# Unit 0 of an attention and gated-MLP kernel: first loads on one queue, products of ones between its blocks, the last blocks scaled on VectorE, zeros beside k written first

## The chip, the cores and the metric

The kernel runs on one NeuronCore of a Trainium2 chip. The metric is the device time of one execution in microseconds, lower is better. Five engines have a queue of their own each and work in the order of that queue: TensorE (PE, with its weight loads shown as PEld), VectorE (DVE), ScalarE (ACT), GpSimd (POOL) and SyncE (SP), which here only issues DMAs. They wait for each other through semaphores. DMAs run beside them; in this kernel they are issued from SP and, at the start, from ACT.

## The reference

Windowed attention over 8 batches, 8 heads, 576 positions and head size 64 (heads 0 to 3 with a plain window of 32, heads 4 to 7 with the same window dilated by 4), and then an RMS norm and a gated MLP (512 to 1536 to 512) over all 4608 positions.

```python
scores = scale * np.matmul(q, k.transpose(0, 1, 3, 2))
scores = np.where(masks[None], scores, -1e9)
attn = np.exp(scores - scores.max(-1, keepdims=True))
attn_out = np.matmul(attn / (attn.sum(-1, keepdims=True) + 1e-9), v)
...
xn = x / np.sqrt(np.mean(x * x, -1, keepdims=True) + 1e-6) * rms_g
g, val = xn @ w_gate, xn @ w_val
out = (g / (1 + np.exp(-g)) * val) @ w_out
```

## The kernel before

The 4608 positions are cut into 16 units of 288 (half a batch). A unit's attention is 14 blocks `(c, i)`: `c` is a pair of heads (0 and 1 plain with 3 blocks each, 2 and 3 dilated with 4 each). A block needs, in this order, the scores `s` (PE, line 417 for units 0 and 1), their mask and row minimum (DVE, 312), the exponentials (ACT, 322), the reciprocal of the sum (DVE, 329 and 330), the scaling of both heads' rows (POOL, 332), a transposition `t` (PE, 394), its copy `pt` to SBUF (ACT, 374), the product with v, `o` (PE, 403), and a copy of that into `xraw` (ACT or DVE, 347). After a pair's last block, ACT squares `xraw` (355), POOL multiplies it by the norm's gain `gs` (357), and the squares are added (361). Behind the unit's last pair come the mean of the squares on PE (`rps`, 458), its root on DVE and POOL (465, 466), a diagonal matrix of it (490), and its spread over the partitions on PE (`bps`, 500), copied as `root` (505); the normalised rows `xn` (511) feed the MLP.

The order on every engine is written out by hand. The main function counts steps in `now`; `later(dt, rank, fn)` puts a piece of work off by `dt` steps, and `flush()` issues a step's pieces by rank. Unit 0's attention takes 25 steps ahead of the main loop (`for n in range(ends)`, lines 674 to 685): step n issues `t` of block n-4, `o` of block n-6 and `s` of block n, in this order on PE. So the transposition of block (1,1) stands in step 8, that of (3,2) in step 16 and that of (3,3) in step 17. From step 19 on the MLP's first products stand between them (`FIRST`, lines 39 and 681). The main loop then has 36 parts for each unit (12 columns of the hidden layer by gate, value and output product), with the next unit's attention in between.

Beside the attention the weights are decoded. They arrive as 36 pieces of 64-bit numbers (`raw_g`, `raw_v`, `raw_o`, 512 KB each, line 124), of which `NRAW` = 4 buffers hold what is under way. Each piece takes one conversion on ACT (135) and three operations on DVE (139, 142, 146), and then its buffer takes the next piece. The table `STEPS` (line 37) says how many of the 108 DVE operations each of the 25 first steps issues; the main loop issues three in each part until none is left.

q, k and v of unit 0 are loaded at the start, by `load(0, h)` for 8 heads (lines 639 and 640): q of a pair as one DMA (207), k of each head (212), v of a pair (218). The pairs 0 and 2 are loaded from SP's queue, the pairs 1 and 3 from ACT's, and behind them on ACT's the gain `gs` (641). The four first weight pieces follow on SP (642, 643). k of a head is padded with zeros in the other head's 64 partitions; a memset (211) does that just ahead of each k's load, on DVE for unit 0 and on POOL for unit 1, whose loads come at the steps 15, 19, 23 and 27.

DMAs from SP and ACT share eight completion counters, taken in turn. A DMA waits, at its place in the queue of its engine, until the earlier one with its counter has landed.

Of the kernel before, what the change touches and what calls it, by code (L numbers as in the profile page):

```python
# [9 lines left out]
F32 = mybir.dt.float32  # L10
# [4 lines left out]
ALU = mybir.AluOpType  # L15
PSUM = bass.MemoryType.PSUM

B, H, S, D = 8, 8, 576, 64
DM, FF = 512, 1536
NT = B * S  # L20
P = 128
U = S // 2
# [4 lines left out]
NC = DM // P  # L27
NJ = FF // P
NNAT = 2
NRAW = 4  # L30
KW = DIL * (U // DIL + W)
# [2 lines left out]


LAG, OUT, LATER = 4, 2, 1
STEPS = (0,) * 5 + (1,) + (2,) * 11 + (1, 1, 0, 0, 0, 1, 1, 1)
SPLITS = 30
FIRST = {19: (("g", 0), ("g", 1)), 20: (("g", 2),), 22: (("g", 3), ("v", 0), ("v", 1)),
         23: (("v", 2), ("v", 3))}  # L40
# [4 lines left out]
def geometry(u, c):  # L45


    half = u % 2
    if c < NC // 2:
        if half:  # L50
            return [(QB * i, QB * i, 0, P) for i in range(U // QB)], QB, U + W
        return [(QB * i, max(QB * i - W, 0), 0 if i else W, P if i else QB)
                for i in range(U // QB)], QB, U
    nq = U // DIL
    keys = nq + (W if half else 0)
    return [(nq * r, keys * r, 0 if half else W, keys) for r in range(DIL)], nq, keys * DIL
# [3 lines left out]
def attn_moe(ctx: ExitStack, tc: tile.TileContext, qk_in, v_in, w_gate, w_val, w_out, rms_g, outT):  # L60
# [3 lines left out]
    nc = tc.nc  # L64
    V, A, G, PE = nc.vector, nc.scalar, nc.gpsimd, nc.tensor

    cst = ctx.enter_context(tc.tile_pool(name="cst", bufs=1))
    sb = ctx.enter_context(tc.tile_pool(name="sb", bufs=2))
    ps = ctx.enter_context(tc.tile_pool(name="ps", bufs=1, space=PSUM))
# [6 lines left out]
    ones = cst.tile([P, P], F32R, name="ones")  # L76
# [11 lines left out]
    gs = cst.tile([P, NC], F32, name="gs")  # L88
# [9 lines left out]
    def later(dt, rank, fn):  # L98
        put_off.setdefault(now[0] + dt, []).append((rank, fn))

    def flush():
        for _, fn in sorted(put_off.pop(now[0], []), key=lambda e: e[0]):
            fn()
# [12 lines left out]
    def load_piece():  # L116
        n = state["loaded"]
        if n == len(pieces):
            return
        state["loaded"] += 1  # L120
        kind, j = pieces[n]
        raw = wp.tile([P, NC, P, 2], U32, tag="raw", name=f"raw_{kind}{j}", bufs=NRAW)
        src = {"g": w_gate, "v": w_val, "o": w_out}[kind][j]
        nc.sync.dma_start(out=raw.rearrange("p c f t -> p (c f t)"), in_=src)
        raws[n] = raw
# [34 lines left out]
    def decode(k):  # L160

        for _ in range(k):
            later(0, 5, step)
        if k:
            later(0, 5.2, ahead)
# [23 lines left out]

    heads, vs, late = {}, {}, []  # L190

    def load(u, h):


        c, a = divmod(h, 2)
        _, _, nkt = geometry(u, c)
        if u >= NNAT:
            raw = sb.tile([P, U + KW], F32, tag="qk", name=f"qk_{u}_{h}", bufs=2)
            nc.sync.dma_start(out=raw[:, :U + nkt], in_=qk_in[u, h][:, :U + nkt])
            heads[u, h] = raw  # L200
            return
        n = 4 * (u * NC + c)
        queue = A if u == 0 and c % 2 else nc.sync
        own, other = (slice(D), slice(D, P)) if a == 0 else (slice(D, P), slice(D))
        if a == 0:
            q = cst.tile([P, U], F32, tag=f"hi{n}", name=f"q_{u}_{c}")
            queue.dma_start(out=q, in_=qk_in[u, h:h + 2, :D, :U])
        else:
            q = heads[u, h - 1][0]
        k = cst.tile([P, KW], F32, tag=f"hi{n + 1 + a}", name=f"k_{u}_{h}")  # L210
        (G if u else V).memset(k[other, :nkt], 0.0)
        queue.dma_start(out=k[own, :nkt], in_=qk_in[u, h][own, U:U + nkt])
        heads[u, h] = q, k
        if a:
            blocks, _, _ = geometry(u, c)
            rows, cols = max(b[3] for b in blocks), len(blocks) * 2 * D
            vt = cst.tile([P, DIL, 2, D], F32, tag=f"hi{n + 3}", name=f"v_{u}_{c}")
            queue.dma_start(out=vt[:rows].rearrange("p i a d -> p (i a d)")[:, :cols],
                              in_=v_in[u, c][:rows, :cols])
            for i in range(len(blocks)):  # L220
                vs[u, c, i] = vt[:, i]
# [103 lines left out]
    def scores_norm(u, c, i):  # L325
        blocks, nq, _ = geometry(u, c)
        n = blocks[i][3]
        t, sm = st[u, c, i]
        V.tensor_scalar(out=sm[:nq, 2:4], in0=sm[:nq, 2:4], scalar1=1e-9, scalar2=None, op0=ALU.add)
        V.reciprocal(out=sm[:nq, 2:4], in_=sm[:nq, 2:4])  # L330
        for a in range(2):
            G.tensor_scalar(out=t[:nq, a, :n], in0=t[:nq, a, :n], scalar1=sm[:nq, 2 + a:3 + a],  # L332
                            scalar2=1.0, op0=ALU.mult, op1=ALU.mult)

    def take(u, c, i, o):

# [26 lines left out]
    def bursts(u):  # L363
        return [(u, c, i) for c in range(NC) for i in range(len(geometry(u, c)[0]))]
# [90 lines left out]
    def rms_sum(u):  # L455
        r_ps = ps.tile([QB, NB, 2], F32, tag="o", name=f"rps_{u}")
        for i in range(NB):
            PE.matmul(r_ps[:, i, :], xsq[u][:, i * QB:(i + 1) * QB], inv, start=True, stop=True)
        later(1, 0.1, lambda: rms_root(u, r_ps))
        if u == 0:  # L460
            later(1, 6, spread_first)
# [34 lines left out]
    def rms_apply(u):  # L496
        ds = rst.pop(u)
        b_ps = ps.tile([P, U], F32, tag="o", name=f"bps_{u}")
        for k, d in enumerate(ds):
            PE.matmul(b_ps, (ones if u else ones32)[:QB, :], d.rearrange("p i q -> p (i q)"),  # L500
                      start=k == 0, stop=k == len(ds) - 1)
        xs[u] = {}
        if u == 0:
            root.append(sb.tile([P, U], F32, tag="tmp", name="root", bufs=2))
            later(1, -1, lambda: A.copy(out=root[0], in_=b_ps))

        def normal(c):
            x = xraw[u, c]
            if u == 0:
                xn = sb.tile([P, U], F32, tag="xhi", name=f"xn_{c}", bufs=4)  # L510
                V.tensor_tensor(out=xn, in0=x, in1=b_ps, op=ALU.mult)
                xs[u][c] = xn
                return
            V.scalar_tensor_tensor(out=x, in0=x, scalar=gs[:, c:c + 1], in1=b_ps,  # L514
                                   op0=ALU.mult, op1=ALU.mult)

        def part(c):
            x = xraw.pop((u, c))
            k = (u * NC + c) % 6
            pool, bufs = (sb, 4) if k < 4 else (late[0], 2)  # L520
            hi = pool.tile([P, U], F32R, tag="xhi", name=f"xhi_{u}_{c}", bufs=bufs)
            lo = late[0].tile([P, U], F32R, tag="xlo", name=f"xlo_{u}_{c}", bufs=6)
            A.copy(out=hi, in_=x)
            (V if c % 2 else G).tensor_tensor(out=lo, in0=x, in1=hi, op=ALU.subtract)
            xs[u][c] = (hi, lo)

        for c in range(NC):
            later((1, 2, 2, 3)[c] if u else 1 + c // 2, 0.6, lambda c=c: normal(c))
            if u:
                later((2, 3, 4, 5)[c], 0.6, lambda c=c: part(c))  # L530
# [18 lines left out]
    def start(kind, c):  # L549

        if kind not in first:
            first[kind] = ps.tile([P, 512], F32, tag={"g": "acc1", "v": "acc3"}[kind], name=f"{kind}_0_0")
        three(first[kind][:, :U], weight(kind, 0, 0), c, xraw[0, c], c == 0, c == NC - 1)
# [82 lines left out]

    nb = len(bursts(0))
    ctx.enter_context(tc.manual_schedule())
    for h in range(H):
        load(0, h)  # L640
    A.dma_start(out=gs, in_=rms_g.rearrange("(c p) -> p c", p=P))
    for n in range(NRAW):
        load_piece()
    for h in range(H):
        later(15 + 4 * (h // 2), 9, lambda h=h: load(1, h))

# [9 lines left out]
    def attend(t_ps, **tags):  # L656
        e = events.pop(now[0], {})
        if any(k in e for k in "qto"):
            products(e.get("q"), e.get("t"), e.get("o"), t_ps, **tags)
        if "sum" in e:  # L660
            rms_sum(e["sum"])
        if "apply" in e:
            rms_apply(e["apply"])
# [10 lines left out]
    for n in range(ends):  # L674
        decode(STEPS[n])
        flush()
        t_ps = None
        if "t" in events.get(n, {}):
            t_ps = ps.tile([P, 512], F32, tag="gv"[n % 2], name=f"t_first_{n}")[:, :2 * QB]
        attend(t_ps, s_tag=("s", "acc0", "acc1", "acc3")[n % (4 if n < nb else 2)], o_tag=("o", "acc2")[n % 2])  # L680
        for kind, c in FIRST.get(n, ()):
            start(kind, c)
        if n == ends - 1:
            _, v_free = gate(0, 0), val(0, 0)
        now[0] += 1

    prev = None
    for u in range(NU):
        for j in range(NJ):
            for part in range(0 if u + j else 2, 3):  # L690
                t = 3 * (u * NJ + j) + part
# [94 lines left out]
```

## Time and profile before

| | us |
|---|---|
| median of 3 runs (lowest, highest) | 1195.87 (1193.26, 1196.34) |
| the profiled execution | 1192.86 |
| its span, first to last instruction | 1190.7 |
| PE busy, share of the span | 1140.4, 96% |
| DVE busy | 755.1, 63% |
| ACT busy | 676.4, 57% |
| POOL busy | 640.8, 54% |

In the lines quoted from the profile, a timeline row gives the start and the length in us, the engine, the line of the kernel, the operation with output and input tile, the shape, how many instructions were merged, and in brackets how long the engine was idle before it and what ended that. The engines SPq and ACTq stand for the issue of DMAs in the queues of SP and ACT. A row of a table by windows gives, for a stretch of time, its length and the busy time of each engine (with the number of instructions), then the clock granted to TensorE, the mean busy share of the 16 DMA engines, and GB/s.

### The profile page before, as it was taken

The numbers are of one execution on the slowest core, as the hardware profiler recorded it, in microseconds if no ns is written. First come the engines' busy times: TensorE is split into PE (matmuls) and PEld (weight loads), VectorE is DVE, ScalarE is ACT, GpSimd is POOL, SyncE is SP. The second block draws the span as 40 slices with busy tenths as digits, with TensorE's granted clock in tenths as the row PEclk, the third lists the DMA queues.
The fourth block names the chain that finished last, engine by engine and source line by source line (L and its number), as shares of the span: only waits on it lengthen the run. The fifth ranks groups of instructions, "written<-read, shape, count | busy, mean of one in ns | idle before, by whom it ended". The sixth has DMA issues, their size and how long they took to land.

```text
span 1190.7 us, 26009 instructions
## 1 busy us (share of the span) xinstructions
PE 1140.4 (96%) x8492; PEld 1103.2 (93%) x8492; DVE 755.1 (63%) x2715; ACT 676.4 (57%) x2456; POOL 640.8 (54%) x1094
## 2 busy tenths in 40 slices
PE   4788899999999999999999999999999999999998
PEld 3566688999999999999999999999999999999998
DVE  4789786765658576665857656585765757575321
ACT  4567576564646556474656646465665646565221
POOL 2666476664646555464655655465555645565211
PEclk9999899999999999999999999999999999999999
DMA  4555321121213112121312212131221213120000
GB/s 151 188 186 188 106 82 50 58 80 32 77 38 92 45 51 80 35 81 36 90 40 70 68 30 78 38 101 38 68 61 35 81 37 93 40 77 16 1 21 20
DMA packets 62711, 82.19 MB, mean 69 GB/s; under 512 B 7442, under 2 KB 43282, under 8 KB 62578
## 3 DMA queue, kind: packets, MB, share of 16 engines
q1 hardware_dynamic: 61242, 79.60, 21.9%
q8 instruction: 68, 1.11, 0.4%
q10 hardware_dynamic: 1336, 0.94, 0.3%
q14 instruction: 65, 0.53, 0.1%
HBM read 71.08 MB, written 9.44 MB: 68 GB/s over the span
## 4 chain that ended last, share of the span: by engine, by line
PE 78%; DVE 14%; DMA 2%; ACT 2%; issue 2%; POOL 1%; SPq 0%; POOLq 0%; DVEq 0%
PE acc L543 8%; PE acc L544 7%; PE acc L545 7%; PE v L543 7%; PE g L543 7%; PE v L544 7%; PE v L545 7%; PE g L544 7%; PE g L545 7%; PE s L420 3%; DVE qs L290 3%; PE g L394 2%; PE o L408 2%; PE o L409 2%; DVE xraw L514 2%
## 5 line engine op out<-in xcount | busy, mean ns | idle before, releaser
L607 POOL TENSOR_TENSOR hlo<-th,hhi 128x288 fp32r<-128x288 f32 x180 | 145.4, 808 | 218.3 <-ACT hhi L606 214.2
L332 POOL TENSOR_SCALAR t<-t,sm 96x128 f32<-96x128 f32 (+3 forms) x448 | 185.2, 425 | 99.4 <-DVE sm L330 74.1
L543 PE MATMUL v<-xhi,hi_v 128*128 128x288 f32 x720 | 220.3, 306 | 3.5 <-DVE pl L378 3.2
L543 PE MATMUL acc<-hhi,hi_o 128*128 128x288 f32 x720 | 221.1, 307 | 0.0
L543 PE MATMUL g<-xhi,hi_g 128*128 128x288 f32 x720 | 219.8, 305 | 0.0
L544 PE MATMUL acc<-hlo,hi_o 128*128 128x288 f32 x720 | 212.8, 295 | 0.2 <-POOL hlo L607 0.2
L544 PE MATMUL g<-xlo,hi_g 128*128 128x288 f32 x720 | 212.9, 296 | 0.0
L544 PE MATMUL v<-xlo,hi_v 128*128 128x288 f32 x720 | 212.8, 296 | 0.0
L545 PE MATMUL acc<-hhi,lo_o 128*128 128x288 f32 x720 | 212.6, 295 | 0.0
L545 PE MATMUL g<-xhi,lo_g 128*128 128x288 f32 x720 | 212.6, 295 | 0.0
L545 PE MATMUL v<-xhi,lo_v 128*128 128x288 f32 x720 | 212.3, 295 | 0.0
L322 ACT ACTIVATE t<-t,sm 96x128 f32<-96x128 f32 (+3 forms) x448 | 166.7, 375 | 18.4 <-DMA k<-in_qk_dram 13.6
L251 POOL TENSOR_TENSOR vlo<-vt,vhi 128x128 fp32r<-128x128 f32 x196 | 98.5, 502 | 125.2 <-ACT vhi L247 109.3
L577 ACT ACTIVATE th<-g 128x288 f32<-128x288 f32 x180 | 74.0, 411 | 157.7 <-PE g L545 106.2
L606 ACT CAST hhi<-th 128x288 fp32r<-128x288 f32 x180 | 78.0, 433 | 141.2 <-DVE th L595 137.2
L543 PEld LDWEIGHTS v<-xhi,hi_v 128*128 128x128 f32 x720 | 135.3, 188 | 6.5 <-DVE pl L378 6.5
L307 DVE TENSOR_TENSOR t<-s,mask 96x256 f32<-96x256 f32 (+3 forms) x196 | 72.0, 367 | 106.7 <-PE s L420 101.1
L544 PEld LDWEIGHTS acc<-hlo,hi_o 128*128 128x128 f32 x720 | 135.8, 189 | 0.5 <-POOL hlo L607 0.5
L544 PEld LDWEIGHTS g<-xlo,hi_g 128*128 128x128 f32 x720 | 135.7, 188 | 0.1
L544 PEld LDWEIGHTS v<-xlo,hi_v 128*128 128x128 f32 x720 | 135.7, 188 | 0.0
L543 PEld LDWEIGHTS acc<-hhi,hi_o 128*128 128x128 f32 x720 | 135.5, 188 | 0.0
L543 PEld LDWEIGHTS g<-xhi,hi_g 128*128 128x128 f32 x720 | 135.3, 188 | 0.2 <-issue 0.2
(120 smaller groups left out, 2662.0 us busy)
## 6 DMA issues: line engine op xcount, KB each, us to landing
qk<-in_qk_dram SPq DMA_DIRECT2D x56, 288.0 KB, 2.9
vt<-in_v_dram SPq DMA_DIRECT2D x196, 64.0 KB, 1.8
qk<-in_qk_dram SPq DMA_DIRECT2D x28, 352.0 KB
out_dram<-ot SPq DMA_DIRECT2D x64, 144.0 KB, 1.9
qk<-in_qk_dram SPq DMA_DIRECT2D x28, 304.0 KB, 2.7
raw_g<-in_w_gate_dram SPq DMA_DIRECT2D x12, 512.0 KB, 3.1
raw_v<-in_w_val_dram SPq DMA_DIRECT2D x12, 512.0 KB, 4.0
raw_o<-in_w_out_dram SPq DMA_DIRECT2D x12, 512.0 KB
```

Of the source, the lines that this page charges most:

```text
L251: G.tensor_tensor(out=vl, in0=vs.pop(b), in1=vh, op=ALU.subtract)
L290: eq.tensor_tensor(out=qs[D:], in0=qr[D:], in1=qs[D:], op=ALU.subtract)
L307: V.tensor_tensor(out=t[:nq, :, :n], in0=sv[:nq, :, 1, :n], in1=mask[:nq, None, mc:mc + n].to_broadcast([nq, 2, n]), op=ALU.add)
L322: A.activation(out=t[:nq, a, :n], in_=t[:nq, a, :n], func=AF.Exp, scale=-1.0, bias=sm[:nq, a:a + 1], accum_out=sm[:nq, 2 + a:3 + a])
L332: G.tensor_scalar(out=t[:nq, a, :n], in0=t[:nq, a, :n], scalar1=sm[:nq, 2 + a:3 + a], scalar2=1.0, op0=ALU.mult, op1=ALU.mult)
L420: PE.matmul(sv[:nq, a, :, :n], qs[:, qc:qc + nq], ks[:, :, kc:kc + n], start=True, stop=True)
L543: PE.matmul(out, wh[:, cc, :], xh, start=start, stop=False)
L544: PE.matmul(out, wh[:, cc, :], xl, start=False, stop=False)
L545: PE.matmul(out, wl[:, cc, :], xh, start=False, stop=stop)
L577: A.activation(out=t, in_=g, func=AF.Tanh, scale=0.5)
L606: A.copy(out=hi, in_=t)
L607: G.tensor_tensor(out=lo, in0=t, in1=hi, op=ALU.subtract)
```

## The change

Five things change, all of them in or ahead of unit 0's attention:

- All of q, k and v of unit 0 is loaded from SP's queue, in the order of the pairs, and `gs` behind the four first weight pieces.
- The zeros beside k of units 0 and 1 are written ahead of all loads, by a function `zeros`; on DVE for unit 0 and on POOL for unit 1 as before.
- A function `busy(n)` issues n products of a 128x128 tile of ones with 512 columns of it (float32r) into a PSUM tile that nobody reads: 7 ahead of the first scores, and 3 in each of the steps 0 to 17, behind that step's scores. The scores' PSUM tiles rotate among three instead of four, since the fourth now takes these products.
- For unit 0's blocks (3,1), (3,2) and (3,3) the scaling is done on DVE instead of POOL.
- `STEPS` issues no decoding in step 5 (one operation before), one in step 17, none in step 18 (one before); so 26 operations are done in the 25 steps, where 28 were.

```diff
-STEPS = (0,) * 5 + (1,) + (2,) * 11 + (1, 1, 0, 0, 0, 1, 1, 1)
+STEPS = (0,) * 6 + (2,) * 11 + (1, 0, 0, 0, 0, 1, 1, 1)
+BUSY = 7, 3
...
+    def zeros(u, h):
+        c, a = divmod(h, 2)
+        k = cst.tile([P, KW], F32, tag=f"hi{4 * (u * NC + c) + 1 + a}", name=f"k_{u}_{h}")
+        (G if u else V).memset(k[(1 - a) * D:(2 - a) * D, :geometry(u, c)[2]], 0.0)
+        zeroed[u, h] = k
...
-        queue = A if u == 0 and c % 2 else nc.sync
...
-            queue.dma_start(out=q, in_=qk_in[u, h:h + 2, :D, :U])
+            nc.sync.dma_start(out=q, in_=qk_in[u, h:h + 2, :D, :U])
...
-        (G if u else V).memset(k[other, :nkt], 0.0)
-        queue.dma_start(out=k[own, :nkt], in_=qk_in[u, h][own, U:U + nkt])
+        k = zeroed.pop((u, h))
+        nc.sync.dma_start(out=k[own, :nkt], in_=qk_in[u, h][own, U:U + nkt])
...
-            G.tensor_scalar(out=t[:nq, a, :n], in0=t[:nq, a, :n], scalar1=sm[:nq, 2 + a:3 + a],
-                            scalar2=1.0, op0=ALU.mult, op1=ALU.mult)
+            (V if u == 0 and (c, i) > (NC - 1, 0) else G).tensor_scalar(
+                out=t[:nq, a, :n], in0=t[:nq, a, :n], scalar1=sm[:nq, 2 + a:3 + a],
+                scalar2=1.0, op0=ALU.mult, op1=ALU.mult)
...
+    for u in range(NNAT):
+        for h in range(H):
+            zeros(u, h)
     for h in range(H):
         load(0, h)
-    A.dma_start(out=gs, in_=rms_g.rearrange("(c p) -> p c", p=P))
     for n in range(NRAW):
         load_piece()
+    nc.sync.dma_start(out=gs, in_=rms_g.rearrange("(c p) -> p c", p=P))
+    busy_ps = ps.tile([P, 512], F32, tag="acc3", name="busy")
+    def busy(n):
+        for _ in range(n):
+            PE.matmul(busy_ps, ones, ones[:, None, :].to_broadcast([P, 4, P]), start=True, stop=True)
+    busy(BUSY[0])
...
-        attend(t_ps, s_tag=("s", "acc0", "acc1", "acc3")[n % (4 if n < nb else 2)], o_tag=("o", "acc2")[n % 2])
+        attend(t_ps, s_tag=("s", "acc0", "acc1")[n % (3 if n < nb else 2)], o_tag=("o", "acc2")[n % 2])
+        if n < nb + LAG:
+            busy(BUSY[1])
```

On ACT the start reads as follows before the change. The names end in a running number that the build gives; `t_0_1` is block (0,1), `pt` a transposed block, `f_g` and `f_v` weight pieces under conversion, `raw_g` and `raw_v` what was loaded.

```order
L212 DMA k_3_108<-in_qk_dram 64x288
L218 DMA v_1_111<-in_v_dram 128x384
L207 DMA q_3_123<-in_qk_dram 128x1x288
L212 DMA k_6_125<-in_qk_dram 64x288
L212 DMA k_7_128<-in_qk_dram 64x288
L218 DMA v_3_131<-in_v_dram 72x512
L641 DMA gs<-in_rms_g_dram 128x4x1
L322 ACTIVATE t_0_0_145,sm_0_0_146<-t_0_0_145,sm_0_0_146 96x96 x2
```

After the change ACT's queue, from its third row on, holds this:

```order
L330 ACTIVATE t_0_0_172,sm_0_0_173<-t_0_0_172,sm_0_0_173 96x96 x2
L330 ACTIVATE t_0_1_182,sm_0_1_183<-t_0_1_182,sm_0_1_183 96x128 x2
L330 ACTIVATE t_0_2_198,sm_0_2_199<-t_0_2_198,sm_0_2_199 96x128 x2
L383 COPY pt_0_0_233<-t_first_220 96x192
L330 ACTIVATE t_1_0_214,sm_1_0_215<-t_1_0_214,sm_1_0_215 96x96 x2
L383 COPY pt_0_1_254<-t_first_241 128x192
L330 ACTIVATE t_1_1_235,sm_1_1_236<-t_1_1_235,sm_1_1_236 96x128 x2
L136 ACTIVATE f_g_262<-raw_g_149 128x512
L136 ACTIVATE f_v_266<-raw_v_151 128x512
L383 COPY pt_0_2_283<-t_first_268 128x192
```

No DMA is left on ACT, and the conversions of the first two weight pieces stand behind the copy of block (0,1) and the exponentials of (1,1); before, they stood ahead of both (behind the exponentials of (1,0)).

On PE the steps 8 and 9 of unit 0's attention now read as follows; before, they were the same rows without those of `busy`.

```order
L403 MATMUL t_first_327<-ident,t_1_1_235 128x96 x2
L412 MATMUL o_0_2_329<-pt_0_2_283,v_0_129 128x192
L426 MATMUL s_2_2_328<-k_4_101,q_2_137 72x72
L426 MATMUL s_2_2_328<-k_5_103,q_2_137 72x72
L661 MATMUL busy<-ones 128x512 x3
L403 MATMUL t_first_356<-ident,t_1_2_256 128x96 x2
L412 MATMUL o_1_0_358<-pt_1_0_313,v_1_135 128x192
L426 MATMUL s_2_3_357<-k_4_101,q_2_137 72x72
L426 MATMUL s_2_3_357<-k_5_103,q_2_137 72x72
L661 MATMUL busy<-ones 128x512 x3
```

Three products that wait for nothing stand behind each step's scores and ahead of the next step's transposition.

On POOL the end of unit 0's attention reads as follows before the change (`xraw` and `sq` are a pair's output and its squares, `k` the padded keys of unit 1).

```order
L332 TENSOR_SCALAR t_3_1_382<-t_3_1_382,sm_3_1_383 72x72 x2
L361 TENSOR_TENSOR sq_0_331<-sq_0_331,sq_1_415 128x288
L332 TENSOR_SCALAR t_3_2_409<-t_3_2_409,sm_3_2_410 72x72 x2
L211 MEMSET k_0_470 64x320
L211 MEMSET k_1_473 64x320
L332 TENSOR_SCALAR t_3_3_439<-t_3_3_439,sm_3_3_440 72x72 x2
L357 TENSOR_SCALAR xraw_2_406<-xraw_2_406,gs 128x288
```

After the change DVE holds the scaling, right behind its own reciprocals:

```order
L337 TENSOR_SCALAR sm_3_2_470<-sm_3_2_470 72x2
L338 RECIPROCAL sm_3_2_470<-sm_3_2_470 72x2
L340 TENSOR_SCALAR t_3_2_469<-t_3_2_469,sm_3_2_470 72x72 x2
L147 SCALAR_TENSOR_TENSOR f_o_447<-raw_o_389,f_o_447 128x512
L143 SCALAR_TENSOR_TENSOR f_g_480<-raw_g_418,f_g_480 128x512
L337 TENSOR_SCALAR sm_3_3_505<-sm_3_3_505 72x2
L338 RECIPROCAL sm_3_3_505<-sm_3_3_505 72x2
L340 TENSOR_SCALAR t_3_3_504<-t_3_3_504,sm_3_3_505 72x72 x2
```

The scaling of the last three blocks has left POOL's queue for DVE's, and the memsets of unit 1's keys have left their place ahead of block (3,3) on POOL.

More of the change, by code (lines that the diff above doesn't have):

```diff
@@ L190, in attn_moe @@
     heads, vs, late = {}, {}, []
+    zeroed = {}
+    def zeros(u, h):
[3 more added lines that the diff above has]
+        zeroed[u, h] = k
     def load(u, h):
@@ L202, in load @@
         n = 4 * (u * NC + c)
-        queue = A if u == 0 and c % 2 else nc.sync
-        own, other = (slice(D), slice(D, P)) if a == 0 else (slice(D, P), slice(D))
+        own = slice(a * D, (a + 1) * D)
         if a == 0:
             q = cst.tile([P, U], F32, tag=f"hi{n}", name=f"q_{u}_{c}")
-            queue.dma_start(out=q, in_=qk_in[u, h:h + 2, :D, :U])
+            nc.sync.dma_start(out=q, in_=qk_in[u, h:h + 2, :D, :U])
         else:
             q = heads[u, h - 1][0]
-        k = cst.tile([P, KW], F32, tag=f"hi{n + 1 + a}", name=f"k_{u}_{h}")
-        (G if u else V).memset(k[other, :nkt], 0.0)
-        queue.dma_start(out=k[own, :nkt], in_=qk_in[u, h][own, U:U + nkt])
+        k = zeroed.pop((u, h))
+        nc.sync.dma_start(out=k[own, :nkt], in_=qk_in[u, h][own, U:U + nkt])
         heads[u, h] = q, k
@@ L217, in load @@
             vt = cst.tile([P, DIL, 2, D], F32, tag=f"hi{n + 3}", name=f"v_{u}_{c}")
-            queue.dma_start(out=vt[:rows].rearrange("p i a d -> p (i a d)")[:, :cols],
+            nc.sync.dma_start(out=vt[:rows].rearrange("p i a d -> p (i a d)")[:, :cols],
                               in_=v_in[u, c][:rows, :cols])
```

## The prediction

> **What bounds the kernel now.** I read the table by windows first, cut where the chain of waits changes its character. Columns: window, length, busy us of PE, PEld, DVE, ACT and POOL, granted clock, DMA share, GB/s.
>
> ```profile
> 8.90:22.75 13.85, 7.25 (x33) 6.53 (x34) 4.03 (x32) 4.17 (x18) 2.11 (x6) 1.00 0.70 227
> 22.75:41.05 18.30, 14.89 (x69) 11.64 (x67) 16.88 (x79) 17.26 (x71) 14.77 (x21) 1.00 0.46 153
> 41.05:55.56 14.51, 12.16 (x37) 9.17 (x38) 7.56 (x23) 4.61 (x15) 8.28 (x14) 1.00 0.66 209
> 55.56:138.56 83.00, 67.26 (x329) 51.44 (x327) 77.00 (x190) 52.49 (x157) 51.53 (x48) 0.99 0.55 177
> 160.00:1190.70 1030.70, 1017.38 (x7931) 1006.94 (x7929) 633.05 (x2340) 584.79 (x2159) 549.92 (x974) 1.00 0.19 55
> ```
>
> From 160 us on PE is busy for 1017.38 of 1030.70 us, with work that the change doesn't touch; this stage only starts earlier or later. From 55.56 to 138.56 DVE sets the pace (77.00 of 83.00). The change acts ahead of 55.56: up to 22.75 all engines wait for loads, from there to 41.05 DVE and ACT are nearly full, and from 41.05 to 55.56 none but PE is.
>
> The first stage, from the timeline:
>
> ```profile
> 8.92 3.65 PE L417 MATMUL s<-k,q 128*96 128x96 f32 x16 [8.92 <-DMA k<-in_qk_dram]
> 16.88 0.40 ACTq L641 DMA_DIRECT2D gs<-in_rms_g_dram  x1
> 17.34 0.37 ACT L322 ACTIVATE t<-t,sm 96x96 f32<-96x96 f32 x1 [13.57 <-DMA k<-in_qk_dram]
> 21.16 0.69 ACT L135 ACTIVATE f_g<-raw_g 128x512 f32<-128x512 f32 x1
> 22.75 0.68 ACT L135 ACTIVATE f_v<-raw_v 128x512 f32<-128x512 f32 x1 [0.91 <-DMA raw_v<-in_w_val_dram]
> 24.31 0.30 ACT L374 COPY pt<-t_first 128x192 f32<-128x192 f32 x1
> 26.68 0.77 PE L394 MATMUL t_first<-ident,t 96*128 96x96 f32 x2 [0.67 <-POOL t L332]
> ```
>
> The first exponential starts at 17.34 although its scores are there by about 10: six DMA issues stand ahead of it on ACT, the last at 16.88. A second gate follows: ACT waits for `raw_v` until 22.75.
>
> **The change part by part.**
>
> *A, loads on one queue.* The first gate goes; the attention can start with its first scores. But the second gate stays, since the conversions of the first two weight pieces now stand behind `pt` of (0,1) and the exponentials of (1,1), and everything after them on ACT waits for the same `raw_v`. When does that land?
>
> ```profile
> 6.00:8.00 2.00, 0.00 (x0) 0.00 (x0) 0.00 (x0) 0.00 (x0) 0.00 (x0) 1.00 0.14 49
> 14.88 0.36 SPq L124 DMA_DIRECT2D raw_g<-in_w_gate_dram  x1
> ```
>
> From 6 to 8 us, with eight loads issued and nothing computed, the DMA share is 0.14: about 2.2 of 16 engines work. So some loads keep a few DMA engines busy while the rest are idle, and the others queue behind them there. One queue instead of two changes the order on those engines, not their bytes: I take `raw_v` to land when it did, within 1 us either way (0.91, the wait that it ended, is the nearest row).
>
> [...]
>
> With `raw_v` at 22.75, `f_v` ends at 23.43 and `pt` of (0,2) follows at once, instead of at 24.31: 0.9 us. For the transposition of (1,1) the path is shorter: `f_g` at 21.16 + 0.69, then two DVE operations on it, two small ones, POOL's scaling, about 2.5 us in all: 24.3 instead of 26.68, so 2.4. Between these I take **A = -1.7**, bounds -3.5 (`raw_v` a microsecond earlier, 2.4 + 1) and +0.5 (a microsecond later, and the cost under C).
>
> *B, scaling on DVE, memsets first.*
>
> ```profile
> 42.06 0.16 DVE L330 RECIPROCAL sm<-sm 72x2 f32<-72x2 f32 x1
> 42.49 0.77 POOL L211 MEMSET k<- 64x320 f32 x2
> 43.26 1.35 POOL L332 TENSOR_SCALAR t<-t,sm 72x72 f32<-72x72 f32 x2
> 44.20 0.80 PE L394 MATMUL t_first<-ident,t 72*72 72x72 f32 x2 [0.79 <-POOL t L332]
> ```
>
> Block (3,3)'s reciprocals are ready at 42.22. Then POOL does memsets and scales until 44.61. On DVE the two scalings follow at 42.2. Their price isn't in the trace; it lies between a small one and a long one of the same kind:
>
> ```profile
> 18.20 0.17 DVE L329 TENSOR_SCALAR sm<-sm 96x2 f32<-96x2 f32 x1 [6.84 <-ACT t L322]
> 21.88 0.43 DVE L139 TENSOR_SCALAR f_g<-f_g 128x512 uint32<-128x512 uint32 x1 [0.29 <-ACT f_g L135]
> ```
>
> 72 columns are nearer the first: 0.2 us each, so 42.6 instead of 44.6: 2.0 gained. Six such operations put 1.2 us (bounds 1.0 and 2.6) on DVE; the four of (3,1) and (3,2) fall where DVE is nearly full, but they also spare a wait of 2.11 us for POOL (below), so I charge 0.5. **B = -1.5**, bounds -2.2 and 0. The memsets at the start cost nothing: the 8 on POOL, 0.77 for two, are over by about 6 us, and the row from 6 to 8 above shows POOL and DVE idle.
>
> *C, the products of ones.* The page's clock column reads 1.00 up to 55, yet the products' own lengths double there:
>
> ```profile
> 46.34 0.82 PE L403 MATMUL o<-pt,v 72*128 72x144 f32 x2 [0.29 <-DVE xraw L347]
> 46.95 3.09 PE L540 MATMUL g<-xraw,f_g 128*128 128x288 f32 x6
> 49.84 1.06 PE L417 MATMUL s<-k,q 128*96 128x128 f32 x4
> 50.69 1.01 PE L458 MATMUL rps<-inv,sq 128*96 128x2 f32 x6
> 51.56 1.31 PE L540 MATMUL g<-xraw,f_g 128*128 128x288 f32 x2
> 52.66 2.13 PE L540 MATMUL v<-xraw,f_v 128*128 128x288 f32 x4
> 54.58 0.94 PE L500 MATMUL bps<-rd,ones 96*128 96x288 f32 x2
> 56.33 0.60 PE L417 MATMUL s<-k,q 128*96 128x128 f32 x4
> 59.75 2.11 PE L540 MATMUL g<-xn,f_g 128*128 128x288 f32 x8
> ```
>
> Six records of `g` took 3.09 us at 46.95, eight took 2.11 at 59.75; the same scores took 1.06 and then 0.60. So PE runs at half pace until about 55, and got its pace only after some 8 us of work without a gap (46.95 to 55). The attention ahead, PE busy 14.89 of 18.30, did not bring it about.
>
> Cost: at full pace 772 products of at most 288 columns take 99.20 us.
>
> ```profile
> 200.00:300.00 100.00, 99.20 (x772) 97.94 (x771) 64.84 (x232) 59.16 (x212) 58.08 (x101) 1.00 0.18 53
> 42.19 0.63 PE L394 MATMUL t_first<-ident,t 72*72 72x72 f32 x2 [2.11 <-POOL t L332]
> ```
>
> That is 128 ns, or 0.23 us for 512 columns: three take 0.69 us at full pace, 1.37 at half. A step lasts (42.19 - 26.68) / 8 = 1.94 us, and PE's own work in it is 14.89 / 18.30 of that, 1.58. Half pace: 1.58 + 1.37 = 2.95, so PE is busy without a gap, which is what brought the pace before; then 0.79 + 0.69 = 1.48, under 1.94. The fill pays for itself if PE speeds up within a few steps.
>
> [...]
>
> [...]
>
> ```profile
> 138.56 1.09 PE L458 MATMUL rps<-inv,sq 128*96 128x2 f32 x6 [4.39 <-DVE sq L361]
> 139.51 4.19 PE L540 MATMUL g<-xn,f_g 128*128 128x288 f32 x8
> ```
>
> After 4.39 idle us eight records take 4.19. So from step 8 on PE starts at half pace and loses 1.0 us per step for two steps, most of it while ACT and DVE work off what waited (in A's bounds).
>
> What full pace is worth: on the chain of waits the rows from 46.95 to 55.56 follow each other on PE. At full pace they halve, 8.6 to 4.3, unless another path ends later:
>
> ```profile
> 48.45 0.46 DVE L361 TENSOR_TENSOR sq<-sq,sq 128x288 f32<-128x288 f32 x1 [0.66 <-ACT sq L355]
> 51.98 0.87 POOL L466 TENSOR_TENSOR rst<-rst,mhalf 96x3 f32<-96x3 f32 x1 [2.18 <-DVE rst L465]
> 52.88 0.46 DVE L490 TENSOR_TENSOR rd<-ident,rst 96x288 f32<-96x288 f32 x1 [0.23 <-POOL rst L466]
> 55.56 0.40 ACT L505 COPY root<-bps 128x288 f32<-128x288 f32 x1 [6.58 <-PE bps L500]
> ```
>
> One does: squares done at 48.9, `rps` 0.6, the root about 1.2 with its first operation, the diagonal 0.5, `bps` 0.6, semaphores: `root` at about 52.0 instead of 55.56, 3.6 gained. The transpositions and outputs ahead (0.80, 1.27, 0.82 us) give another 0.4. **C = -4.0**, bounds -5 and -2 (if pace is lost between the last fill and 46.95).
>
> *D, two decode operations later.* They go to the stage that DVE bounds, at 0.43 to 0.7 us each; of 108 the last now stands behind the sum of squares ahead of `rps` at 138.56, so one counts. **D = +0.7**, bounds +0.6 and +1.4.
>
> Sum: -1.7 - 1.5 - 4.0 + 0.7 = **-6.5 us**; all bounds together -10.1 and -0.1. DVE was idle 6.95 us from 41.05 to 55.56, so it has room for B and C, 5.5, and not for much more. The stage after 55.56 is bound by DVE's work and shifts as a whole. The profiled execution took 1192.86 us, 2.10 more than its span, and would become 1186.4. It lies 3.0 below the median of the runs, 1195.87, from which I count: **1189.4 us**.
>
> **The rivals.**
>
> *PE never gets its pace* (the other side). If the products of ones, with the waits for POOL between them, do not count as the gapless work of 46.95 to 55, ten steps (8 to 17) cost 2.95 instead of 1.94: +10.1, less A and B, plus D: +7.6, 1203.5 us. It decides at whether PE is still at half pace three steps after the loads. For it: 81% busy was not enough before. Against: at 2.95 nothing else can hold PE up. 10%.
>
> *The weights keep the old schedule.* If the stage from 55.56 is set by the arrival of weight pieces rather than by DVE, its end stays put and only D or a little of A shows: -2 to +1.4, about 1195.5. For it: the DMA share of 0.55 and ACT's waits for pieces. Against: DVE's 77.00 of 83.00. The same comes out if a late `raw_v` eats A and DVE fills up in the tail. 20%.
>
> *More than the sum.* `raw_v` lands a microsecond early, because the tiny packets of `gs` no longer precede it, and PE catches up at once: about -10, 1186. 12%.
>
> *The change doesn't do what it says* only for the 7 first products, whose pace is lost again by 22 us; that is in the sum.
>
> **How the numbers follow.** The forecast, -4 to -9, has 58%. About 3.6 us (0.3%) is what a measurement of this kernel can tell from no change. Faster: 58 + 12 = 70%; within 0.3%: 20%; slower: 10%. The range reaches from the large gain, 1184, to the case without gain, 1196; beyond lie the slower rival and a little on the low side.
>
> **What would show it.** Right: the first exponential before 10 us; `f_v` on ACT still at 21.5 to 23.5 with a wait for `raw_v`; scores of 128 columns at 0.6 per four from about step 11; no wait of `t` for POOL in steps 16 and 17; `root` at 47 to 50; `rps` of unit 1 at 131 to 133.5 instead of 138.56. Wrong: full-length products at step 12 (the slower rival), `root` early but `rps` at 138 (the weights), or `f_v` at 25 or later (one queue is slower than two).

## The result, and the profile after

| | before | after |
|---|---|---|
| median (lowest, highest), us | 1194.62 (1193.26, 1196.34) | 1205.94 (1200.98, 1206.84) |
| the profiled execution, us | 1192.86 | 1200.98 |
| its span, us | 1190.7 | 1199.0 |

Four runs each; the ratio is 1.0086, 95% interval 1.0059 to 1.0113. The forecast was 1189.4: the kernel became slower by about 10 us, where a gain of 6.5 was expected. The profiled execution is the fastest of the four, 8.1 us longer than the one before; the other three, with a granted clock of 0.981 to 0.984 where it has 0.990, took 1205.52 to 1206.84, and what they lost beyond it is in no profile.

The same two views as in the prediction, the timeline and the table by windows, on the changed kernel (its lines stand 1 to 9 further down: conversions of a weight piece at 136, `rps` at 467, `root` at 514). Rows of the timeline from the first 25 us:

```profile
8.24 0.38 ACT L330 ACTIVATE t<-t,sm 96x96 f32<-96x96 f32 x1 [5.93 <-DVE sm L320]
22.31 0.67 ACT L136 ACTIVATE f_v<-raw_v 128x512 f32<-128x512 f32 x1 [0.60 <-DMA raw_v<-in_w_val_dram]
24.69 0.77 PE L403 MATMUL t_first<-ident,t 96*128 96x96 f32 x2 [5.34 <-POOL t L340]
```

The first exponential comes at 8.24 instead of 17.34, the second gate (`raw_v`) is where it was, and the transposition of (1,1) starts at 24.69 instead of 26.68. The end of unit 0's attention, in the same view:

```profile
43.41 0.33 PE L403 MATMUL t_first<-ident,t 72*72 72x72 f32 x2 [0.57 <-DVE t L340]
46.40 0.66 ACT L136 ACTIVATE f_g<-raw_g 128x512 f32<-128x512 f32 x1 [1.94 <-DMA raw_g<-in_w_gate_dram]
47.41 0.51 PE L412 MATMUL o<-pt,v 72*128 72x144 f32 x2 [1.92 <-ACT pt L383]
47.76 1.62 PE L549 MATMUL g<-xraw,f_g 128*128 128x288 f32 x6
53.02 0.40 ACT L514 COPY root<-bps 128x288 f32<-128x288 f32 x1 [3.91 <-PE bps L509]
146.60 1.09 PE L467 MATMUL rps<-inv,sq 128*96 128x2 f32 x6 [4.46 <-DVE sq L370]
```

The products at 47.76 run at full pace (six in 1.62, before in 3.09), and `root` comes at 53.02 instead of 55.56. But unit 1's `rps` starts at 146.60 instead of 138.56. So 2.5 us were won ahead of the main loop, and 10.6 were lost in the stage behind it (93.6 instead of 83.0 us). From there on the two profiled executions don't differ: from `rps` to the end of the span it is 1052.4 us, before 1052.1.

What is late in that stage? The table by windows, columns as in the prediction:

```profile
53.02:146.60 93.58, 71.49 (x328) 54.94 (x327) 70.36 (x192) 52.92 (x158) 48.73 (x46) 0.94 0.52 165
```

DVE, which was to set the pace with 77.00 of 83.00, is now busy for 70.36 of 93.58. It waits for ACT: ahead of `h` (line 582, after the change 591), DVE's idle time that ends with work of ACT grows from 0.6 to 13.7 us. The chain of waits from 50 to 150 us tells what ACT waits for (start, length, engine, tile and line; `...` stands for rows left out):

```profile
67.78 6.86 DMA raw_g<-in_w_gate_dram
74.65 0.66 ACT f_g L136
76.75 0.76 DVE f_o L140
...
80.84 3.13 DMA raw_g<-in_w_gate_dram
84.00 0.68 ACT f_g L136
86.97 0.69 DVE f_v L147
87.67 0.60 DVE f_o L143
89.25 0.60 ACT hi_o L187
90.40 5.07 DMA raw_g<-in_w_gate_dram
95.49 0.66 ACT f_g L136
```

A weight piece is issued (67.78), ACT reaches its conversion before it has landed (74.64), and DVE follows. In the groups of lines, ACT's waits for pieces from 50 to 150 us (busy, mean ns | idle ahead, and what ended most of it), before:

```profile
L135 ACT ACTIVATE f_o<-raw_o 128x512 f32<-128x512 f32 x9 | 6.1, 677 | 11.0 <-DMA raw_o<-in_w_out_dram 11.0
L135 ACT ACTIVATE f_g<-raw_g 128x512 f32<-128x512 f32 x8 | 5.4, 679 | 1.5 <-DMA raw_g<-in_w_gate_dram 1.4
L135 ACT ACTIVATE f_v<-raw_v 128x512 f32<-128x512 f32 x8 | 5.4, 670 | 5.9 <-DMA raw_v<-in_w_val_dram 5.9
```

and after:

```profile
L136 ACT ACTIVATE f_o<-raw_o 128x512 f32<-128x512 f32 x9 | 6.1, 681 | 17.2 <-DMA raw_o<-in_w_out_dram 17.2
L136 ACT ACTIVATE f_v<-raw_v 128x512 f32<-128x512 f32 x9 | 6.1, 675 | 6.3 <-DMA raw_v<-in_w_val_dram 6.3
L136 ACT ACTIVATE f_g<-raw_g 128x512 f32<-128x512 f32 x8 | 5.4, 671 | 10.8 <-DMA raw_g<-in_w_gate_dram 10.6
```

18.3 us of waiting became 34.1. The pieces, their size and their DMAs are the same.

**The theory tested below, PHASE.** In the main loop three decode operations are issued in each part. With 28 of the 108 done ahead of it, a part holds low of piece n, shift of n+1, sign of n; with 26 it holds shift of n, sign of n-1, low of n. The sign operation frees a buffer and issues the next load. `ahead()`, at a part's end, issues the conversion of the piece that is at most one beyond the piece of the next operation, if its load has been issued. Followed through the code, that puts the conversion of a piece two parts behind the issue of its load with 28, and one part behind with 26. ACT works in the order of its queue, so a conversion that comes before its data holds up the tanh, the exponentials and the copies behind it: the one at 74.65 had waited 5.65 us for `raw_g`, and behind it, from 75.72 to 77.52, came a tanh (line 586), the copies `pt` and `xraw` and two exponentials.

### The profile page after: what moved, and what is told of

Its sections match the earlier page's. It is cut to its first block, busy times and chain, and to the rows that moved or that the text cites. A ratio compares the mean times of both kernels' runs of the same rounds, so it can differ in the third digit from the quotient of the medians.

```text
span 1199.0 us, 26139 instructions
## 1 busy us (share of the span) xinstructions
PE 1149.6 (96%) x8553; PEld 1109.2 (93%) x8553; DVE 749.1 (62%) x2721; ACT 676.9 (56%) x2456; POOL 632.0 (53%) x1088
## 4 chain that ended last, share of the span: by engine, by line
PE 75%; DVE 14%; DMA 5%; ACT 2%; issue 2%; POOL 1%; SPq 0%; POOLq 0%; DVEq 0%
PE acc L552 8%; PE v L552 7%; PE acc L553 7%; PE acc L554 7%; PE g L552 7%; PE v L553 7%; PE v L554 7%; PE g L553 7%; PE g L554 7%; DMA raw_g<-in_w_gate_dram 3%; DVE qs L298 3%; PE s L429 3%; DVE xraw L523 2%; PE g L403 2%; PE o L417 2%
## 5 line engine op out<-in xcount | busy, mean ns | idle before, releaser
L340 POOL TENSOR_SCALAR t<-t,sm 72x104 f32<-72x104 f32 (+3 forms) x442 | 175.5, 409 | 87.7 <-DVE sm L338 67.4
L615 ACT CAST hhi<-th 128x288 fp32r<-128x288 f32 x180 | 78.0, 433 | 142.7 <-DVE th L604 137.4
```

The source lines that it names most:

```text
L340: (V if u == 0 and (c, i) > (NC - 1, 0) else G).tensor_scalar(out=t[:nq, a, :n], in0=t[:nq, a, :n], scalar1=sm[:nq, 2 + a:3 + a], scalar2= ...
L615: A.copy(out=hi, in_=t)
```

## Experiments: the loss

Each ratio below is to the kernel before, run beside it on the same chip, with its 95% interval; `root`, `rps` (of unit 1) and the stage between them are from the profiled execution. The executions of one and the same kernel lie up to 6.3 us apart, so a microsecond or two between two such single profiles can be chance.

**28 operations again.** All else stays changed.

```diff
-STEPS = (0,) * 6 + (2,) * 11 + (1, 0, 0, 0, 0, 1, 1, 1)
+STEPS = (0,) * 5 + (1,) + (2,) * 11 + (1, 1, 0, 0, 0, 1, 1, 1)
```

> The changed kernel with STEPS as it was (28 decode operations ahead of the main loop instead of 26); loads, products of ones, scaling and memsets stay changed. Theory PHASE (with 26 operations a part of the main loop holds shift of piece n, sign of n-1, low of n, and ACT's conversion of a piece stands one part behind the issue of its load; with 28 it stands two parts behind): the stage from `root` to unit 1's `rps` goes back from 93.6 to 82-85 us, waits of `f_g` for `raw_g` on ACT from 50 to 150 us fall from 10.6 to under 3, unit 1's `rps` starts at 135-138, and the time is 1189-1193 against 1194.6 before. Rival LOADS OR PRODUCTS (one queue, the fill or the memsets have delayed the weight pieces): the stage stays at 91 or more and the time at 1202 or more. Rival COUNT (each operation fewer costs DVE time later): the stage becomes shorter by two operations only, about 1.4 us, and the time is 1203-1205.

Measured: ratio 0.9999 (0.9989 to 1.0010), `root` 54.95, `rps` 137.84, stage 82.9, ACT's waits for `raw_g` 3.0. The loss is gone with the table. The gain isn't there either; that is the second question below.

**The new table alone,** in the kernel before (the same lines the other way).

> The kernel before with only the new STEPS (26 operations instead of 28). PHASE: the stage from `root` to unit 1's `rps` grows from 83.0 to 91-95 us and the time is 1202-1206, all of the loss and without any of the gain of the start. COUNT: +0.7 to +1.4 us, 1195.3-1196. LOADS OR PRODUCTS: no more than +1.4 either.

Measured: 1.0078 (1.0062 to 1.0095), 1201.33 us, a little below the expected time; `root` 56.64, `rps` 149.57, stage 92.9. The table alone makes the loss, without any of the other four edits. The rivals COUNT and LOADS OR PRODUCTS fall.

**25 operations:** one fewer still, in the phase of 28.

```diff
-STEPS = (0,) * 6 + (2,) * 11 + (1, 0, 0, 0, 0, 1, 1, 1)
+STEPS = (0,) * 6 + (2,) * 11 + (1, 0, 0, 0, 0, 0, 1, 1)
```

> The changed kernel with one decode operation fewer still (25: none in step 22). 25 has the same remainder by three as 28, so the conversions stand two parts behind the issue of the loads again. PHASE: stage from `root` to unit 1's `rps` 83-87 us, time 1190-1195. COUNT: a longer stage than with 26 operations, time 1206-1209. LOADS OR PRODUCTS: unchanged from the changed kernel, 1204-1208.

Measured: 0.9996 (0.9984 to 1.0007), `root` 53.56, `rps` 137.44, stage 83.9. With less done ahead, the stage is 9.7 us shorter than with 26.

**Conversions held back one part,** in the main loop of the changed kernel; the table stays at 26.

```diff
-        if ops and n <= ops[0][1] + 1 and n in raws:
+        if ops and n <= ops[0][1] + (now[0] < ends) and n in raws:
```

> The changed kernel, STEPS and DVE's order unchanged (26 operations); in the main loop only, the conversion of a piece on ACT is issued one part later. PHASE, with the place of the conversions on ACT as its mechanism: ACT's waits for `raw_g`, `raw_v`, `raw_o` from 50 to 150 us fall from 34 to under 20, the stage becomes 83-87 us, the time 1190-1195. If it is the order of DVE's operations itself (sign behind shift) or the later issue of the loads, with the conversions innocent: stage 91 or more, time 1203-1207.

Measured: 0.9991 (0.9979 to 1.0003), `root` 55.25, `rps` 138.45, stage 83.2; ACT's waits for pieces 14.0 us. DVE's order is that of the changed kernel, so that order by itself is not the cause.

**Conversions one part earlier,** in the kernel before, with nothing of the change in it.

```diff
-        if ops and n <= ops[0][1] + 1 and n in raws:
+        if ops and n <= ops[0][1] + 1 + (now[0] >= ends) and n in raws:
...
             later(0, 5.2, ahead)
+            if now[0] >= ends:
+                later(0, 5.2, ahead)
```

> The kernel before, STEPS and DVE's order as they are, nothing of the change; in the main loop only, the conversion of a piece is issued one part earlier, so that it stands one part behind the issue of its load, as it came to stand in the changed kernel. PHASE: ACT's waits for pieces from 50 to 150 us grow from 18.3 to about 34 us, the stage from 83.0 to 90-94, unit 1's `rps` at 146-150, time 1199-1204 against 1192.3. If the conversions' place matters little and the rest (DVE's order, loads) made the loss: stage below 86, time under 1196.

Measured: 1.0094 (1.0078 to 1.0110), 1205.35 us; `rps` at 150.06, ACT's waits for pieces 33.7 us; time and stage a little beyond what PHASE expected. Its stage by windows:

```profile
54.11:150.06 95.95, 71.52 (x328) 53.95 (x327) 69.86 (x190) 52.26 (x157) 48.73 (x48) 0.95 0.47 154
```

This is the picture of the changed kernel: DVE at 69.86 of 95.95, and PE at a clock of 0.95 (0.76 from 70 to 80 us, where it is busy for only 3.80 of 10). The place of the conversions is shown as the cause from both sides: moved back it mends the changed kernel, moved forward it breaks the one before.

## Experiments: where the gain went

The kernels with the right phase should have won about 7 us (A, B and C). They won next to nothing. What follows keeps the 26 operations and the held conversions, except where said.

**Held from step 17 on.** The wait at 46.40 above stands ahead of the copy `pt` of (3,3).

```diff
-        if ops and n <= ops[0][1] + 1 and n in raws:
+        if ops and n <= ops[0][1] + (now[0] < 17) and n in raws:
```

> As the run that holds the conversions back in the main loop, but held from step 17 on, so that the conversion of the second gate piece no longer stands on ACT ahead of the copy `pt` of block (3,3). Four kernels with the right phase all reached unit 1's `rps` between 137.4 and 138.6, with `root` anywhere from 53.0 to 55.6. Theory START (the stage shifts with `root`, the start just gained too little: the wait for `raw_g` ahead of `pt`, and PE falling back to half clock behind it): output product of (3,3) at 45.2-46.2 instead of 47.0, `root` at 51-53, unit 1's `rps` at 135-136.8, time 1189-1191 against 1192.4 before. Rival WEIGHTS (the stage ends when the weight pieces are through, whenever `root` comes): `root` early, `rps` at 137.4-138.6, time 1191.5-1193.

Measured: 0.9984 (0.9971 to 0.9996). The MLP's products behind the output of (3,3) start at 46.64 instead of 47.33, `root` comes at 53.56, `rps` at 137.78, with PE at half pace from 44 to 50 in the profiled execution (granted clock 0.50 from 45 to 48). `rps` is where WEIGHTS put it, but `root` is later than the 51 to 53 of START, so it decides between them only weakly. The profiled execution is the longest of the twelve, 1193.42 us at a granted clock of 0.987; the shortest took 1187.96 at 0.994.

**And three products in step 18** (`if n < nb + LAG + 1: busy(BUSY[1])`).

> The same with three more products of ones in step 18, between the output products of (3,2) and (3,3), where PE was idle for 1.8 us. START, with the clock as its second half: PE's granted clock stays at 1.00 from 31 to 56 us, `root` at 51-52.5, `rps` at 135-136.5, time 1188.5-1190.5. WEIGHTS: `rps` at 137.4-138.6, time 1191.5-1193. If the products only cost: `root` 0.7 later than without them.

Measured: 0.9979 (0.9968 to 0.9989). The clock stayed at 1.00 from 41 to 55 (six products of `g` took 1.62 us, in the run before 3.09), `root` came at 51.58 and `rps` at 134.83, outside the 137.4 to 138.6 of WEIGHTS: an earlier `root` does carry through.

**Products of ones alone,** in the kernel before: the two lines with `busy`, 7 and 3, and the scores on three PSUM tiles.

> The kernel before with only the products of ones (7 ahead, 3 in each of the steps 0 to 17, scores on three PSUM tiles). Step C by itself, as forecast: `root` 3-4 us earlier than 55.56. START: `root` at 51.5-53.5, `rps` at 135-137, time 1189-1191. WEIGHTS: `rps` at 137.4-138.6, time 1191.5-1193. If PE falls back to half clock in its gaps in this order too: `root` 54-56, time 1192-1193.

Measured: 0.9994 (0.9983 to 1.0006). `root` at 52.58, 3.0 early, but `rps` at 137.20: the stage took 84.6. C by itself moves `root` within its bounds, but the time doesn't show its gain.

**No products** (`BUSY = 0, 0`), with conversions held in the main loop only, and then from step 17 on.

> The changed kernel with conversions held back in the main loop and without any product of ones (steps A, B and D, with the phase mended). Forecast for A and B: 3.2 us at `root`, less 1.1 for the wait for `raw_g` ahead of `pt`: `root` at 53-54 with the tail at half pace, `rps` 136-137.5 (START) or 137.4-138.6 (WEIGHTS), time 1190-1192. If the products held PE up rather than helped it: `root` earlier than 53.

> The changed kernel without any product of ones and with the conversions held back from step 17 on: steps A and B alone, without the wait for `raw_g` ahead of `pt` of (3,3). Output product of (3,3) at 43.7-44.5 (46.34 before), at half pace from there 9.2 us to `root`: 53.0-53.7. START: unit 1's `rps` at 136-137.2, time 1190-1191.5. If the products' share in the 0.2% gain was all: `root` 54.5 or later, time 1192-1193.

Measured: 0.9982 (0.9973 to 0.9991) and 0.9991 (0.9981 to 1.0000); `root` 55.42 and 52.76, `rps` 138.88 and 137.18. The `rps` of 138.88 is later than either theory put it. The same two kernels with products stand at 0.9991 and 0.9984: in the time the products show no gain. What they cost can be read from the first one's timeline, beside that of the kernel with the fill of step 18. Transpositions of (2,2) and (3,3) without products:

```profile
28.60 0.63 PE L403 MATMUL t_first<-ident,t 72*72 72x72 f32 x2 [0.71 <-POOL t L340]
41.70 0.42 PE L403 MATMUL t_first<-ident,t 72*72 72x72 f32 x2 [0.93 <-DVE t L340]
```

and with them:

```profile
29.97 0.29 PE L403 MATMUL t_first<-ident,t 72*72 72x72 f32 x2
43.08 0.33 PE L403 MATMUL t_first<-ident,t 72*72 72x72 f32 x2 [0.56 <-DVE t L340]
24.00:30.00 6.00, 5.59 (x23) 4.65 (x24) 4.30 (x22) 4.91 (x22) 2.03 (x6) 0.55 0.28 91
```

Both started (1,1) at 24.4. The products of ones cost 1.4 us between (1,1) and (2,2), where PE comes out of its wait at a clock of 0.55 (the row by windows) and is busy for 5.59 of 6 us, and nothing works that off by (3,3).

**A bridge over that wait:** 24 more products in step 7.

```diff
-        if n < nb + LAG:
-            busy(BUSY[1])
+        if n < nb + LAG + 1:
+            busy(BUSY[1] + 24 * (n == 7))
```

> As the run with the fill of step 18, and 24 more products of ones in step 7, to be worked off in the 6.9 us in which PE waits for the transposition of (1,1). Theory COLD FILL (the products of ones that start at half pace behind that wait hold the attention up by 1.4 us: transposition of (2,2) at 29.97 with them and 28.60 without, of (3,3) at 43.08 and 41.70): PE keeps full pace through the wait, transposition of (1,1) stays at 24.2-24.6, that of (2,2) at 28.3-28.8, that of (3,3) at 41.5-42, `root` at 49.8-50.6 instead of 51.58, unit 1's `rps` at 133-134.2, time 1187.5-1189.5. Rival: DVE or ACT set the pace from 24 to 43 in any case: transposition of (3,3) at 43, time 1189.5-1191.

Measured: 0.9973 (0.9963 to 0.9984). The gap is filled, and the pace kept:

```profile
18.24 6.41 PE L661 MATMUL busy<-ones 128*128 128x512 f32 x27
24.49 0.49 PE L403 MATMUL t_first<-ident,t 96*128 96x96 f32 x2
41.61 0.34 PE L403 MATMUL t_first<-ident,t 72*72 72x72 f32 x2 [0.58 <-DVE t L340]
18.00:41.00 23.00, 21.03 (x120) 15.62 (x117) 18.88 (x81) 18.32 (x72) 12.30 (x17) 1.00 0.58 192
41.00:48.00 7.00, 6.10 (x25) 5.02 (x24) 4.32 (x14) 1.85 (x6) 2.57 (x3) 0.76 0.72 215
```

(3,3) is at 41.61, the 1.4 us are back, so COLD FILL is right. But this execution lost the pace from about 42 to 46, and `root` came at 51.32 only, `rps` at 136.18; these and the time, 1190.26 us, are later than expected.

**28 operations, the two extra ones in the steps 20 and 21,** with bridge and fill; conversions held in the steps 17 to 24.

```diff
+STEPS = (0,) * 6 + (2,) * 11 + (1, 0, 0, 1, 1, 1, 1, 1)
...
+        if ops and n <= ops[0][1] + (now[0] < 17 or now[0] >= ends) and n in raws:
```

> As the run that bridges the wait, with 28 decode operations ahead of the main loop again, the two extra ones in the steps 20 and 21, where DVE was idle; conversions held back in the steps 17 to 24 only, since with 28 the main loop has the right phase by itself. Forecast's step D by itself: two operations of 0.43 to 0.7 us less in the stage. D as a count only (0.3 us an operation, from the stages of 82.9 with 28, 83.2 with 26 and 83.9 with 25): unit 1's `rps` 0.6 to 1.4 earlier than 136.2, 134.8-135.6, time 1189-1190 against 1192.3 before. Rival, DVE has room: `rps` at 136-137, time 1190-1191.

Measured: 1189.75 us, ratio 0.9971 (0.9957 to 0.9984). This version beats both kernels. In its profiled execution, the fastest of the twelve at 1187.80, `root` is at 50.41 and `rps` at 133.35, earlier than expected. Its last two stages:

```profile
41.05:50.41 9.36, 7.80 (x39) 5.86 (x40) 7.36 (x23) 2.37 (x7) 4.00 (x4) 1.00 0.75 232
50.41:133.35 82.94, 68.90 (x328) 52.67 (x327) 77.04 (x190) 52.89 (x158) 49.94 (x46) 0.98 0.55 183
```

Full clock through the tail, and DVE at 77.04 of 82.94 again. In time it can't be told from the run before it (0.9973), so the two operations have no price that these runs resolve.

## Why the prediction was wrong

**D failed, and with it the sentence that carried it:** "The stage after 55.56 is bound by DVE's work and shifts as a whole." D counted two operations at 0.7 us, and no run above resolves a price for their number. What the table also sets is in which order the main loop's parts take shift, low and sign, and so how far ACT's conversions run behind the loads. That order depends on the remainder when the number of operations done ahead is divided by three; 28 and 26 differ in it, and this costs +9.3 us by itself (ratio 1.0078 of 1192.4). DVE's 77.00 of 83.00 was read as it stands, but it bounds the stage only as long as pieces are there when ACT asks for them. Nor is all of it fixed work: the changed kernel, with two instructions more in the stage, has DVE busy for 70.36; the eight operations on `sm` of 72x2 (line 329, after the change 337) lasted 774 ns each before and 187 after. Why DVE's instructions are longer where the stage is short was not looked into. ACT's 18.3 us of waits for pieces in the stage were there to be read, and so was the order of the conversions against the loads; the prediction compared both orders only ahead of the main loop.

Of the 17 us between the forecast (6.5 gained) and the result (about 10 lost), D makes up 8.6 (9.3 less the 0.7 charged). Most of the rest is the 7.2 of A to C, of which nothing showed in the time with the old table (ratio 0.9999); the paragraphs on A, B and C say how far that is explained.

**The rivals.** "The weights keep the old schedule" looked at the right resource, the arrival of pieces, but let it hold the end of the stage in place; it moved 8 us later. "PE never gets its pace" had the right size, 1203.5, by a mechanism that the trace refutes: the products at 47.76 ran at full pace, six in 1.62 us.

**A was right at its place:** -2.0 at the transposition of (1,1), within its bounds, with the second gate as foreseen (`f_v` at 22.31). Without products it lasts, with B's, to the transposition of (3,3): 41.70 against 44.20, 2.5 us where A and B were to bring 3.2.

**B was right in price and wrong in what follows.** Two scalings on DVE take 0.42 us for (3,2) and for (3,3), as taken; those of (3,1) took 1.64, so that the six come to 2.48, just inside the upper bound of 2.6. (3,3)'s transposition no longer waits for POOL. But with the new table the conversion of the second gate piece stands on ACT ahead of `pt` of (3,3), and waits for its load until 46.40; the output product came 1.1 us later than before.

**C had the right size where PE kept its pace, and two costs left out.** From that output product to `root` it is 5.6 us instead of 9.2 in the changed kernel's profile: 3.6 gained, as worked out. But the start at half pace behind the wait for `raw_v` (a clock of 0.55 from 24 to 30 us in the run with the fill of step 18), charged to A's bounds as mostly covered, costs 1.4 us in full; and the pace is kept in the tail in some executions and not in others. The changed kernel, and the same with conversions held in the main loop, have the same program up to `root`, and came out so:

```profile
47.00:55.00 8.00, 6.74 (x34) 5.01 (x34) 4.74 (x16) 2.98 (x11) 1.64 (x2) 1.00 0.69 194
```

```profile
47.00:55.00 8.00, 8.00 (x26) 6.31 (x27) 3.22 (x11) 0.83 (x3) 1.65 (x2) 0.57 0.61 197
```

The first had full clock and `root` at 53.02, the second 0.57 and 55.25. The time goes with the clock from one execution to the next in the kernel with 28 operations, bridge and fill too: the executions with a granted clock of 0.995 or 0.996 took 1187.80 to 1189.22 us, the two with 0.992 took 1192.70 and 1194.00.

With the phase right and these holes filled, in that same kernel, `root` moves by 5.15 us and the profiled span by 5.0 (1185.7), the time by 0.29%, about 3.5 us: the gain forecast for A to C, 7.2, is half there.

**What stays open.** An early `root` did not always carry through: in six kernels with the right phase and `root` between 51.3 and 53.6 the stage took 83.3 to 84.9 us, in four with `root` at 54.9 or later (the kernel before among them) 82.9 to 83.5, and in the best one, with `root` at 50.41, 82.9. What makes up this difference of up to 2 us, and how much of it is chance between single executions, wasn't tried, nor were A and B each by itself.

## What to carry to other kernels

Where a fixed number of steps per iteration is taken from a list, changing how many are taken ahead of the loop changes the phase of everything that is tied to the list: follow each load from its issue to its first use, in both orders, inside the loop too. Here the conversions on ACT passed their waits on to what stood behind them in its queue: one part closer to the loads, ACT waited 15.8 us more and the stage grew by 10.6. ACT's busy time in the stage, 52.49 us before and 52.92 after, doesn't show that; the distance between issue and use does.

## What the runs showed of the hardware

PE fell to half pace without a long gap in the run with 28 operations and all else changed. The rows around the fall:

```profile
42.53 0.33 PE L403 MATMUL t_first<-ident,t 72*72 72x72 f32 x2 [0.75 <-ACT f_o L136]
42.93 0.94 PE L661 MATMUL busy<-ones 128*128 128x512 f32 x3
44.19 0.33 PE L403 MATMUL t_first<-ident,t 72*72 72x72 f32 x2 [0.32 <-DVE t L340]
44.85 0.48 PE L412 MATMUL o<-pt,v 72*128 72x144 f32 x2 [0.33 <-DVE xraw L356]
45.08 1.42 PE L661 MATMUL busy<-ones 128*128 128x512 f32 x3
47.75 3.09 PE L549 MATMUL g<-xraw,f_g 128*128 128x288 f32 x6
```

Three products take 0.94 us at 42.93 and 1.42 at 45.08, though no gap between them is longer than 0.33 us, and the one ahead is 0.75 (PE was busy for 1.82 of 3 us from 42 to 45, and for 2.84 of 3 from 45 to 48; the granted clock was 1.00 and then 0.56). Nor does the program alone settle it: the two executions in the section on the prediction, with the same program up to `root`, had a clock of 1.00 and of 0.57 from 47 to 55 us.

A busy share just short of full did not bring the pace in the run without products that held the conversions in the main loop only: PE was busy for 2.87 and then 2.81 of 3 us from 30 to 36, and the granted clock was 0.50 there and stayed so until 55.

Loads waited in their queues until earlier ones had landed. In the kernel before, SP and ACT had issued eight by 3.91 us; ACT's next one came at 8.39, and SP's next at 10.99, after 7.1 us of waiting for a load of `q`.
